# A fused attention and MLP block on one core: requests of the opening in another order, and the first MLP unit's evictions and weight preparation rearranged

## The chip, the cores and the metric

The kernel runs on one core of a Trainium2 chip. The metric is the device time of one execution in microseconds (us), start to end. A core has five instruction streams that run in parallel and meet at semaphores: PE (the matrix engine, with its weight loads listed as PEld), DVE (VectorE), ACT (ScalarE), POOL (GpSimd) and SP (SyncE, which here only issues DMA requests). Each stream issues its own instructions strictly in order: an instruction that waits holds back all that stands behind it on its engine.

## The reference, cut to what matters

The input `A_x` is 2048 rows of 576 columns, float32. Six vectors come from a condition vector `c`; they scale, shift and gate two sub-blocks.

```
mod = (_silu(c) @ w_mod).reshape(c.shape[0], 6, 1, -1)
sa, ca, ga, sb, cb, gb = (mod[:, 0], ..., mod[:, 5])
x = x + ga * _A_ref(_layernorm(x) * (1 + ca) + sa, A_wqkv, A_wo)   # sliding attention, 32 heads, window 256
x = x + gb * _B_ref(_layernorm(x) * (1 + cb) + sb, B_w1, B_w2, B_w3, B_w4)

_B_ref(x):  h  = gelu(layernorm(x) @ w1)              # token mixing
            x1 = x + shifted(h) @ w2
            return x1 + gelu(layernorm(x1) @ w3) @ w4   # channel MLP, 576 -> 4608 -> 576
```

All matrix products are kept near float32 accuracy: each operand is split into a rounded high part and the remainder (low part), and three products (high-high, low-high, high-low) are summed.

## The kernel before

**The order.** The whole program is written as a list of events `at(t, f)`: a number `t` and a function that issues instructions (line 69). `build` sorts the list by `t` and calls the functions in that order (lines 1365 and 1366). The number is only a sort key, not a time on the chip: it decides where the instructions of a function stand in the stream of each engine. Semaphores for the dependences are added by the framework; a tile with `bufs=n` has n buffers in turn, and a write to a reused buffer waits until all readers of the old content are done.

**Opening** (`qkv`, lines 141 to 449). Rows are worked on in four blocks of 512. The first two condition vectors are needed at once (`mod01`); the other four (`modr`, line 222, result `pmr`) are computed while block 0 is on PE, from five tiles `wm` of `w_mod`, 128 x 2304 each, two buffers (`wmload`, line 193; the fifth has 64 rows). They share these two buffers with the tiles `wmf` of `mod01`. For block b, PE computes nine products `qk` of 128 columns each (`fmm`, line 322), 14 matmuls of 512 columns in one of four PSUM banks s0 to s3 in turn. `fev` (line 341) brings each one from PSUM to a tile `qs` (three buffers) with an ACT copy and a DVE subtraction, and `fst` (line 347) stores it to DRAM. On PE, `pmr` of `wm` tile 0 stands between `qk` 4 and `qk` 5 of block 0, that of tile 1 between `qk` 7 and `qk` 8. The weights of Q and K come in three column blocks `raw` (`wload`, two buffers), those of V in two (`vload`, line 271, in the same two buffers, so that the first V load waits until the second block of Q and K weights is split, line 269). All these loads and stores are issued by SP, one behind the other; the rows `x` are loaded by SP from tile 4 on (`xload`, line 157).

**The end of token mixing** (`mixing`, line 983 on; `mix_events`). For each of 16 row tiles t: two products `w` of 288 columns are added to `x1` on DVE (`w2ev`, line 967), the mean and variance are taken on DVE (`st`, result `d{t}mv`), POOL computes the reciprocal root in three small instructions (lines 133 to 136, `d{t}rs`), ACT writes the normalised rows `xm` (line 981), and `rsum` multiplies `x1` by `gb` in place and adds it to the residual `rr`, both on POOL (lines 985 and 986). `rr` is stored to `rd` and comes back later as the start of the MLP's accumulators `acc` (`ainit`, line 1277).

**The MLP** (`mlp`, `mlp_events`). The 4608 hidden columns are taken as 18 units of 2 x 128, first for rows 0 to 1023, then, in reverse, for rows 1024 to 2047. One level of a Strassen-like scheme makes each unit's up-projection seven products instead of eight, in the order P1, P6, P7, P5, P4, P2, P3 (`up`, line 1235), each 7 matmuls of 512 columns. They use banks s0 to s3 in turn, so that P4 needs the bank of P1, P2 that of P6, P3 that of P7, and the next unit's P1 that of P5. P1 is copied to SBUF on ACT (`keep`, line 1212), the others are combined on DVE (`comb`, line 1205: U2 = P6 + U1, U3 = P7 + U2, C22 = P5 + U3, U4 = P5 + U2, C21, C11, C12). Four of them go through gelu and a rounding copy on ACT (lines 1223 and 1225) and a subtraction on DVE (line 1232) to the high and low parts `G`. The down-projection `d` of a unit (line 1255) is interleaved on PE with the next unit's up-projection, and needs `G` and both parts of `W4`.

The weights of unit jj are prepared one unit ahead in one raw tile `wf` with a single buffer, which also holds the rows of `w4` for unit jj-1. In order: nine loads on SP (`wload`, line 1072), four sums on POOL (`wsum`, line 1093), the high parts in two casts on ACT (`whi`, line 1099, slices 0 to 2 and 3 to 6), the low parts in two subtractions on POOL (`wlo`, line 1105) and for a remainder of the rows in two on DVE (`wtail`, line 1113), and for `w4` the multiplication by `gb` on POOL (`w4gb`, line 1119), the cast on ACT (`w4hi`, line 1128) and the low part on POOL (`w4lo`, line 1134). The next `wf` can be loaded only when all of them have read the old one. In `wprep` (line 1137) each has an offset from a start t0 as a fraction of a length dt; for the first two units the events are placed by hand in `mlp_events`:

```
for i, f in enumerate((whi(0, 0, 3), wlo(0, self.nc.gpsimd, 0, 3), whi(0, 3, 7), wlo(0, self.nc.gpsimd, 3, 7))):
    at(Tc + .04 + .01 * i, f)
at(T0 - 7.7, wtail(0, self.nc.vector))
add(wprep(1, 1, 0, T0 - 4.0, 11.0))
```

T0 is the key of the first up-projection, U (24.2) the length of a unit in keys; the first unit's seven products have keys T0 + 0.47 U n / 7.

Of the kernel before, what the change touches and what calls it, by code (L numbers as in the profile page):

```python
# [12 lines left out]
ALU = mybir.AluOpType  # L13
# [7 lines left out]
NT = S // P  # L21
# [12 lines left out]
class Kern:  # L34
# [34 lines left out]
    def at(self, t, f, *a):  # L69
        self.ev.append((t, (lambda: f(*a)) if a else f))  # L70
# [70 lines left out]
    def qkv(self, T0, TB):  # L141
        nc, at, ps = self.nc, self.at, self.ps
# [267 lines left out]
        for b in range(4):  # L410
            t0 = T0 + TB * b
            for f in range(9):
                tf = t0 + fq * f
                if b or f > 2:
                    at(tf, fmm, b, f)
                at(tf + fq + .1, fev, b, f)
                at(tf + fq + 2.0, fst, b, f)
            tv = t0 + 9 * fq
            for i in range(4):
                t = 4 * b + i  # L420
                for r in range(2):
                    at(tv + fv * (i + r / 2), vmm, t, r)
                    at(tv + fv * (i + (r + 1) / 2) + .1, vev, t, r)
                at(tv + fv * (i + 1) + 2.0, vst, t)
            if b == 0:
                at(t0 + 3, wsplit, 2)
                at(t0 + 3.1, vload, 1)
                at(t0 + 7, vsplit, 0, 0)
                at(t0 + 8, vsplit, 0, 1)
                at(t0 + 12, vsplit, 1, 0)  # L430
                at(t0 + 13, vsplit, 1, 1)
                for k in range(5):
                    at(t0 + 4 + 7 * k, wmload, k, 1152, 3456)
                    at(t0 + 16 + 7 * k, modr, k)
                    at(t0 + 17.5 + 7 * k, modre, k)
                at(t0 + 16 + 28 + 4, modst)
            if b < 3:
                for i in range(4):
                    t = 4 * b + 4 + i
                    at(t0 + 2 + i, xload, t)  # L440
                    at(t0 + 14 + 3 * i, st, t)
                    at(t0 + 17 + 3 * i, nrm, t)
                for k in range(5):
                    at(t0 + 31 + 2.5 * k, tr, b + 1, k)
                    at(t0 + 31.6 + 2.5 * k, hev, b + 1, k)
# [360 lines left out]
    def mixing(self, T0, TB):  # L806
        nc, at, ps = self.nc, self.at, self.ps
# [174 lines left out]

        def rsum(t):
            r, x = X["rr", t], X["x1", t]
            nc.gpsimd.tensor_tensor(out=x, in0=x, in1=self.gb, op=ALU.mult)
            nc.gpsimd.tensor_tensor(out=r, in0=r, in1=x, op=ALU.add)

        def xst(t):
            nc.sync.dma_start(self.xmd[t], X["xm", t])
# [5 lines left out]
        for k in range(5):  # L995
# [3 lines left out]
            at(T0 + (8.5, 11, 14.5, 17.7, 22)[k], w2split, k)  # L999
        at(T0 + 24, lambda: nc.sync.dma_start(self.gb, self.modd[5].to_broadcast([P, D])))  # L1000
        return load, tr, tev, w1mm, w1ev, halo, hend, hload, w2mm, w2ev, xpl, st, nrm, rsum, xst, rst

    def mix_events(self, T1, TB, fns):
# [282 lines left out]
    def mlp_events(self, T1, Tc, T0, U, fns):  # L1286
        begin1, begin2, begin3, aload, asum, adup, atr, aev, wload, wsum, whi, wlo, wtail, wprep, w4gb, w4hi, w4lo, ainit, up, down, Ws = fns
        at = self.at
        NJ = F // 2 // P
        SB = S // 1024  # L1290
        B12, B11, B21, B22, T1_, T2, T3, T4 = range(8)
# [8 lines left out]
        add = lambda l: self.ev.extend(l)  # L1300
# [6 lines left out]
        for i, f in enumerate((whi(0, 0, 3), wlo(0, self.nc.gpsimd, 0, 3), whi(0, 3, 7), wlo(0, self.nc.gpsimd, 3, 7))):  # L1307
            at(Tc + .04 + .01 * i, f)
        at(T0 - 7.7, wtail(0, self.nc.vector))
        add(wprep(1, 1, 0, T0 - 4.0, 11.0))  # L1310
        at(T0 + .35, begin3)
        for k in range(8):
            at(T0 + (.2 if k < 5 else .4) * U + .01 * k, ainit(0, (k + 4) % 8))
        t = T0
# [80 lines left out]
```

## Time and profile before

| what | value |
|---|---|
| median of 3 runs | 1800.95 us (1793.26 to 1802.7) |
| the profiled execution's own time | 1797.62 us |
| span of its trace | 1795.5 us |
| mean granted PE clock | 0.98 of full speed |
| opening, up to the last product of block 0 | about 85 us |
| first instruction of the MLP's up-projection on PE | 875.4 us |
| first `d` of the MLP that runs without a break | 899.4 us |

Times in the trace count from the start of the span; the 2.1 us between the span and the execution's own time lie around it. A row of the timeline shows the start, the length, the engine, the line, the operation, output<-input with tile names (buffer numbers left out), shapes and the number of instructions merged in it (x14); in brackets how long the engine had been idle and what ended that. In a row of stretches (windows) stand, for each engine, the busy time and the count, then the granted PE clock, the share of the DMA engines and GB/s. The end of a matmul is modelled; start to start of two rows is the safer measure on PE.

### The profile page before, as it was taken

What the parts mean: (1) busy time and instruction counts of PE and PEld (TensorE: products, weight loads), DVE (VectorE), ACT (ScalarE), POOL (GpSimd) and SP (SyncE); (2) the same over time, 40 slices, a digit from 0 to 9 for tenths busy, and PEclk for the clock granted to TensorE, in tenths of its full rate; (3) what the DMA queues carried; (4) which work ended last, traced back from release to release, by engine and by line L of the source; (5) the groups of instructions that cost most, each with busy time, mean ns of one, the idle gap of its engine ahead of it and who ended that gap; (6) DMA issues with size and microseconds to landing.
All of it is one profiled execution on the core that took longest, in us unless ns stands there. A gap on an engine that the chain in (4) does not pass through costs nothing.

```text
span 1795.5 us, 33620 instructions
## 1 busy us (share of the span) xinstructions
PE 1687.2 (94%) x13369; PEld 1536.9 (86%) x13369; DVE 1105.5 (62%) x1885; ACT 708.4 (39%) x1211; POOL 901.0 (50%) x839
## 2 busy tenths in 40 slices
PE   6999998999999989988799999999989999999998
PEld 4788888888889879988688999999878999999997
DVE  6444255666767637666666666666775666666664
ACT  3222135454544554444334433333433333344331
POOL 4222257545454533464766555556544556655550
PEclk9999999999999999999899999999989999999999
DMA  7755544546455446543422222111233211222211
GB/s 225 277 178 178 173 137 137 146 133 172 129 157 162 140 138 217 196 158 129 158 74 62 62 62 62 48 52 56 62 119 102 62 47 50 59 62 62 62 45 53
DMA packets 156499, 206.77 MB, mean 115 GB/s; under 512 B 19316, under 2 KB 87924, under 8 KB 155768
## 3 DMA queue, kind: packets, MB, share of 16 engines
q1 hardware_dynamic: 153720, 203.19, 36.7%
q8 instruction: 106, 1.74, 0.4%
q10 hardware_dynamic: 2624, 1.45, 0.3%
q14 instruction: 49, 0.40, 0.1%
HBM read 143.76 MB, written 60.56 MB: 114 GB/s over the span
## 4 chain that ended last, share of the span: by engine, by line
PE 74%; DVE 6%; POOL 5%; ACT 5%; issue 4%; DMA 4%; SPq 1%; ACTq 1%; POOLq 0%; DVEq 0%
PE d L1255 24%; PE qk L331 6%; PE X L568 4%; PE mx L519 4%; PE av L607 3%; PE v L369 3%; PE wo L692 3%; PE X L570 2%; PE pg L916 2%; PE w L965 1%; DVE W L1113 1%; ACT avs L612 1%; DMA wmf<-in_w_mod_dram 1%; ACTq L554 1%; DMA wf<-in_B_w_dram 1%
## 5 line engine op out<-in xcount | busy, mean ns | idle before, releaser
L1255 PE MATMUL d<-W,G 128*128 128x288 f32 x3456 | 506.5, 297 | 13.1 <-DVE acc L1263 9.8
L1255 PEld LDWEIGHTS d<-W,G 128*128 128x128 f32 x3456 | 488.3, 189 | 34.9 <-DVE acc L1263 11.0
L1263 DVE TENSOR_TENSOR acc<-d,acc 128x576 f32<-128x576 f32 x288 | 216.9, 754 | 201.3 <-PE d L1255 199.1
L1093 POOL TENSOR_TENSOR wf<-wf 128x384 f32<-128x384 f32 x140 | 144.9, 1055 | 339.8 <-DMA wf<-in_B_w_dram 325.6
L585 ACT ACTIVATE P<-X 128x512 f32<-128x512 f32 (+4 forms) x320 | 177.7, 573 | 195.0 <-PE X L570 153.6
L537 DVE TENSOR_REDUCE m<-mx 128x2 f32<-128x640 f32 x144 | 117.8, 820 | 106.4 <-PE mx L523 105.9
L568 PE MATMUL X<-QD,KS 128*128 128x64 f32 (+2 forms) x704 | 144.7, 298 | 10.6 <-ACT P L585 9.9
L1105 POOL TENSOR_TENSOR W<-wf,W 128x768 fp32r<-128x768 f32 x70 | 152.1, 2194 | 2.7 <-ACT W L1099 2.7
L1232 DVE TENSOR_TENSOR G<-U,G 128x512 fp32r<-128x512 f32 x108 | 91.6, 848 | 100.0 <-ACT G L1225 100.0
L519 PE MATMUL mx<-KD,QS 128*128 128x320 f32 (+4 forms) x512 | 144.3, 342 | 7.0 <-DVE m L537 2.5
L499 POOL TENSOR_SCALAR QS<-QD,rowm 128x512 fp32r<-128x512 f32 x128 | 87.4, 695 | 111.2 <-DMA QD<-qd 73.4
L1223 ACT ACTIVATE U<-U 128x512 f32<-128x512 f32 x108 | 68.5, 634 | 178.6 <-DVE U L1208 178.6
L1223 ACT ACTIVATE C<-C 128x512 f32<-128x512 f32 x36 | 22.8, 634 | 286.4 <-DVE C L1208 286.4
L568 PEld LDWEIGHTS X<-QD,KS 128*128 128x128 f32 x704 | 107.5, 192 | 19.1 <-ACT P L585 16.3
L331 PE MATMUL qk<-hT,Wqk 128*128 128x512 f32 x462 | 110.4, 399 | 1.1 <-DVE qs L345 1.1
L506 POOL TENSOR_SCALAR KS<-KD,rowm 128x768 fp32r<-128x768 f32 (+1 forms) x128 | 109.0, 864 | 0.0
L1119 POOL TENSOR_TENSOR wf<-wf,gb 128x1152 f32<-128x1152 f32 x35 | 104.5, 2985 | 7.1 <-DVE acc L1263 7.1
L331 PEld LDWEIGHTS qk<-hT,Wqk 128*128 128x128 f32 x462 | 87.2, 190 | 24.1 <-DVE qs L345 1.6
L519 PEld LDWEIGHTS mx<-KD,QS 128*128 128x128 f32 x512 | 93.3, 194 | 13.5 <-issue 5.0
L1134 POOL TENSOR_TENSOR W<-wf,W 128x1152 fp32r<-128x1152 f32 x35 | 96.7, 2764 | 6.9 <-ACT W L1128 6.9
L1099 ACT CAST W<-wf 128x1152 fp32r<-128x1152 f32 x70 | 90.1, 1319 | 21.8 <-DMA wf<-in_B_w_dram 10.2
L570 PE MATMUL X<-Mk,identr 128*128 128x256 f32 (+2 forms) x320 | 95.6, 299 | 0.0
(785 smaller groups left out, 3221.6 us busy)
## 6 DMA issues: line engine op xcount, KB each, us to landing
wf<-in_B_w_dram SPq DMA_DIRECT2D x35, 576.0 KB
wf<-in_B_w_dram SPq DMA_DIRECT2D x140, 128.0 KB
KD<-kd SPq DMA_DIRECT2D x72, 216.0 KB
QD<-qd SPq DMA_DIRECT2D x96, 144.0 KB
wf<-in_B_w_dram SPq DMA_DIRECT2D x140, 64.0 KB
qd<-qs SPq DMA_DIRECT2D x16, 512.0 KB
kd<-qs SPq DMA_DIRECT2D x16, 512.0 KB
vd<-Vst SPq DMA_DIRECT2D x16, 312.0 KB
```

Of the source, the lines that this page charges most:

```text
L331: nc.tensor.matmul(po, W[:, a, fs], H[:, c, :], start=(n == 0), stop=(n == 13))
L506: nc.gpsimd.tensor_scalar(t[:, b0:, r], src[:, b0:], M[:, 2 + r:3 + r], 0.0, op0=ALU.mult, op1=ALU.add)
L519: nc.tensor.matmul(pm[:, s, 320 - 64 * nb:320], lhs, K[:, j, 64 * (i + 5 - nb):64 * (i + 5)], start=True, stop=merged(n, j, bb))
L537: nc.vector.tensor_reduce(out=m[:, c:c + 2], in_=pm[:, :, 0:320], axis=mybir.AxisListType.X, op=ALU.max, negate=True)
L568: nc.tensor.matmul(px[:, c:c + q1 - q0], K[:, b + 4].rearrange("p r k -> p (r k)"), Q[:, j, q0:q1], start=(i == 0), stop=False)
L570: nc.tensor.matmul(o, self.identr, mv, start=False, stop=True)
L585: nc.scalar.activation(p[:, lo:], X["px", n, j, k][:, lo:], AF.Exp, scale=SCALE)
L1093: nc.gpsimd.tensor_tensor(out=WF[:, o], in0=WF[:, a], in1=WF[:, b], op=ALU.subtract)
L1105: eng.tensor_tensor(out=W[:, s0:s1, 3:5, :], in0=WF[:, 1 + s0:1 + s1, 0:2], in1=W[:, s0:s1, 0:2, :].bitcast(F32), op=ALU.subtract)
L1119: nc.gpsimd.tensor_tensor(out=R4, in0=R4, in1=gb.unsqueeze(1).to_broadcast([P, 2, D]), op=ALU.mult)
L1255: nc.tensor.matmul(po, G[:, g, ta, b, ts], W[:, w, b, cs], start=(n == 0), stop=(n == 5))
L1263: nc.vector.tensor_tensor(out=a, in0=po, in1=a, op=ALU.add)
```

## The change

Four things, all but one by keys alone. In the opening, the loads of `wm` tiles 0 and 1 and of row tiles 4 and 5 get keys ahead of the V weight loads. In token mixing, `rsum` of row tile 14 runs on DVE. And for MLP unit 1 the call of `wprep` is replaced by events with keys of their own: `keep` of the first product (key T0 + 1.626, unchanged) now comes ahead of the two `whi`, the DVE `wtail` comes behind the second sum U3, and on POOL the two small jobs of row tile 15 and the first `wlo` move ahead of `w4gb`, the second `wlo` ahead of `rsum` of row tile 15. No instruction is added or dropped, and PE's own order does not change.

```diff
                 for k in range(5):
-                    at(t0 + 4 + 7 * k, wmload, k, 1152, 3456)
+                    at(t0 + 4 + 7 * k if k > 1 else -29 + .1 * k, wmload, k, 1152, 3456)
...
-                    at(t0 + 2 + i, xload, t)
+                    at(t0 + 2 + i if t > 5 else -28.9 + .1 * i, xload, t)
...
         def rsum(t):
             r, x = X["rr", t], X["x1", t]
-            nc.gpsimd.tensor_tensor(out=x, in0=x, in1=self.gb, op=ALU.mult)
-            nc.gpsimd.tensor_tensor(out=r, in0=r, in1=x, op=ALU.add)
+            tt = (nc.vector if t == NT - 2 else nc.gpsimd).tensor_tensor
+            tt(out=x, in0=x, in1=self.gb, op=ALU.mult)
+            tt(out=r, in0=r, in1=x, op=ALU.add)
...
         at(T0 - 7.7, wtail(0, self.nc.vector))
-        add(wprep(1, 1, 0, T0 - 4.0, 11.0))
+        at(T0 - 4.0, wload(1, 1, 0))
+        for i, o in enumerate(((T1_, B12, B11), (T2, B22, T1_), (T3, B22, B12), (T4, B21, T2))):
+            at(T0 - 1.8 + .2 * i, wsum(1, *o))
+        pool = self.nc.gpsimd
+        for e, f in ((1.64, whi(1, 0, 3)), (1.66, whi(1, 3, 7)), (1.7, wlo(1, pool, 0, 3)), (1.75, w4gb(0)), (1.8, wlo(1, pool, 3, 7)),
+                     (3.3, w4hi(0)), (3.4, w4lo(0)), (4.9, wtail(1, self.nc.vector))):
+            at(T0 + e, f)
```

The line numbers behind line 984 are higher by one in the new program, those behind line 1310 by seven.

**Opening, SP.** SP's requests from the first V weight load on (`raw_484` or `raw_492`; the last Q and K block stands just ahead of it). Before:

```order
L274 DMA raw_484<-in_A_wqkv_dram 128x4x288
L275 DMA raw_484<-in_A_wqkv_dram 64x288
L276 DMA raw_484<-in_A_wqkv_dram 64x288
L159 DMA x_488<-in_A_x_dram 128x576
L159 DMA x_495<-in_A_x_dram 128x576
L274 DMA raw_497<-in_A_wqkv_dram 128x4x288
L275 DMA raw_497<-in_A_wqkv_dram 64x288
L276 DMA raw_497<-in_A_wqkv_dram 64x288
L195 DMA wm_1152_504<-in_w_mod_dram 128x2304
```

The same place of the changed program:

```order
L195 DMA wm_1152_484<-in_w_mod_dram 128x2304
L195 DMA wm_1152_486<-in_w_mod_dram 128x2304
L159 DMA x_488<-in_A_x_dram 128x576
L159 DMA x_490<-in_A_x_dram 128x576
L274 DMA raw_492<-in_A_wqkv_dram 128x4x288
L275 DMA raw_492<-in_A_wqkv_dram 64x288
L276 DMA raw_492<-in_A_wqkv_dram 64x288
L274 DMA raw_501<-in_A_wqkv_dram 128x4x288
```

Both first `wm` tiles now stand ahead of both V loads; `wm` tile 0 was behind them, and tile 1 five requests further, behind two row tiles and two stores.

**The MLP's first unit, DVE.** From the first half of row tile 15 on (`W_1` is the weight tile of unit 1; `U_0`, `C_0`, `u0P` are sums and products of unit 0). Before:

```order
L969 TENSOR_TENSOR x_15_11684<-w_15_0_11746,x_15_11684 128x288
L969 TENSOR_TENSOR x_15_11684<-w_15_1_11771,x_15_11684 128x288
L130 BN_STATS d15st<-x_15_11684 128x6
L131 BN_STATS d15st<-x_15_11684 128x6
L132 BN_AGGR d15mv<-d15st 128x2
L1113 TENSOR_TENSOR W_1_11635<-wf_11735,W_1_11635 32x7x128 x2
L1208 TENSOR_TENSOR U_0_11850<-u0P_11823,U_0_11831 128x512
L1208 TENSOR_TENSOR U_0_11870<-u0P_11842,U_0_11850 128x512
L1208 TENSOR_TENSOR C_0_11883<-u0P_11862,U_0_11870 128x512
```

After:

```order
L969 TENSOR_TENSOR x_15_11684<-w_15_0_11746,x_15_11684 128x288
L986 TENSOR_TENSOR x_14_11644<-x_14_11644,gb 128x576
L987 TENSOR_TENSOR rr_11651<-rr_11651,x_14_11644 128x576
L969 TENSOR_TENSOR x_15_11684<-w_15_1_11771,x_15_11684 128x288
L130 BN_STATS d15st<-x_15_11684 128x6
L131 BN_STATS d15st<-x_15_11684 128x6
L132 BN_AGGR d15mv<-d15st 128x2
L1209 TENSOR_TENSOR U_0_11846<-u0P_11819,U_0_11827 128x512
L1209 TENSOR_TENSOR U_0_11868<-u0P_11838,U_0_11846 128x512
L1114 TENSOR_TENSOR W_1_11635<-wf_11735,W_1_11635 32x7x128 x2
L1209 TENSOR_TENSOR C_0_11883<-u0P_11860,U_0_11868 128x512
```

The sums U2 and U3 no longer stand behind `wtail`, but C22 does; and the second half of row tile 15 now stands behind `rsum` of tile 14.

**The same stretch, POOL.** From the four `wsum` of unit 1 to `w4lo` of unit 0. Before:

```order
L1093 TENSOR_TENSOR wf_11735<-wf_11735 128x384 x4
L985 TENSOR_TENSOR x_14_11644<-x_14_11644,gb 128x576
L986 TENSOR_TENSOR rr_11651<-rr_11651,x_14_11644 128x576
L1119 TENSOR_TENSOR wf_11735<-wf_11735,gb 128x1152
L133 TENSOR_SCALAR d15rs<-d15mv 128x1
L134 TENSOR_TENSOR d15rs<-d15rs,mhalf 128x1
L136 TENSOR_SCALAR d15rs<-d15mv,d15rs 128x1
L1105 TENSOR_TENSOR W_1_11635<-wf_11735,W_1_11635 128x3x256
L985 TENSOR_TENSOR x_15_11684<-x_15_11684,gb 128x576
L986 TENSOR_TENSOR rr_11701<-rr_11701,x_15_11684 128x576
L1105 TENSOR_TENSOR W_1_11635<-wf_11735,W_1_11635 128x4x256
L1134 TENSOR_TENSOR W_0_11833<-wf_11735,W_0_11833 128x1152
```

After:

```order
L1094 TENSOR_TENSOR wf_11735<-wf_11735 128x384 x4
L133 TENSOR_SCALAR d15rs<-d15mv 128x1
L134 TENSOR_TENSOR d15rs<-d15rs,mhalf 128x1
L136 TENSOR_SCALAR d15rs<-d15mv,d15rs 128x1
L1106 TENSOR_TENSOR W_1_11635<-wf_11735,W_1_11635 128x3x256
L1120 TENSOR_TENSOR wf_11735<-wf_11735,gb 128x1152
L1106 TENSOR_TENSOR W_1_11635<-wf_11735,W_1_11635 128x4x256
L986 TENSOR_TENSOR x_15_11684<-x_15_11684,gb 128x576
L987 TENSOR_TENSOR rr_11701<-rr_11701,x_15_11684 128x576
L1135 TENSOR_TENSOR W_0_11848<-wf_11735,W_0_11848 128x1152
```

The two instructions of tile 14 are gone from POOL, and `w4lo` stands last as before. On ACT, `keep` of unit 0 moves ahead of both `whi` of unit 1, and `xm` of row tile 15 ahead of `w4hi`.

## The prediction

> **What bounds the kernel.** First the shares of the engines and the chain that ended last, from the page:
>
> ```profile
> PE 1687.2 (94%) x13369; PEld 1536.9 (86%) x13369; DVE 1105.5 (62%) x1885; ACT 708.4 (39%) x1211; POOL 901.0 (50%) x839
> PE 74%; DVE 6%; POOL 5%; ACT 5%; issue 4%; DMA 4%; SPq 1%; ACTq 1%; POOLq 0%; DVEq 0%
> ```
>
> PE is busy 94% of the span and carries most of the chain. PE's own work isn't touched, so an edit can gain only where PE stands still or runs at a lower clock. The change touches two such places; everything between and after them follows PE and shifts with it. The first is the opening, PE's timeline:
>
> ```profile
> 38.01 3.54 PE L331 MATMUL qk<-hT,Wqk 128*128 128x512 f32 x14 [1.13 <-DVE qs L345]
> 45.99 2.15 PE L228 MATMUL pmr<-wm,silub 128*32 128x288 f32 x16 [4.44 <-DMA wm<-in_w_mod_dram]
> 48.07 11.12 PE L331 MATMUL qk<-hT,Wqk 128*128 128x512 f32 x42
> 59.12 1.18 PE L228 MATMUL pmr<-wm,silub 128*32 128x288 f32 x16
> 60.23 3.53 PE L331 MATMUL qk<-hT,Wqk 128*128 128x512 f32 x14
> 63.60 2.01 PE L369 MATMUL v<-Wv,hT 128*128 128x288 f32 x14
> ```
>
> Read it start to start: behind `qk` 4 PE stands 4.44 us until `wm` tile 0 has landed, then the first `pmr` takes 2.08 against 1.11 for the second, and `qk` 5 to 7 take 11.05 where `qk` 8 takes 3.37. The stretches give the reason, and SP's timeline why the load is late:
>
> ```profile
> 25.00:30.00 5.00, 5.00 (x23) 4.00 (x23) 3.62 (x5) 4.48 (x6) 3.24 (x3) 1.00 0.00 0
> 46.00:48.10 2.10, 2.10 (x17) 0.62 (x17) 0.00 (x0) 0.00 (x0) 0.00 (x0) 0.50 1.01 363
> 48.10:51.80 3.70, 3.70 (x16) 2.96 (x12) 1.18 (x3) 0.72 (x2) 0.00 (x0) 0.68 1.06 427
> 19.50 1.55 SPq L248 DMA_DIRECT2D raw<-in_A_wqkv_dram  x1
> 32.07 0.37 SPq L274 DMA_DIRECT2D raw<-in_A_wqkv_dram  x1
> 38.98 0.52 SPq L195 DMA_DIRECT2D wm<-in_w_mod_dram  x1
> 40.56 1.42 SPq L352 DMA_DIRECT2D qd<-qs  x2
> ```
>
> After the stall the granted clock is 0.50, then 0.68. SP's last request of the Q and K weights ends at 21.05; then SP stands until 32.07 at the first V load, which waits for its buffer, and the DMA engines are empty (0.00) from 25 to 30. `wm` tile 0 is asked for at 38.98.
>
> The second place is the MLP's first unit: PE, then POOL, DVE, ACT and SP.
>
> ```profile
> 882.66 1.90 PE L1202 MATMUL u0P<-A,W 128*128 128x512 f32 x7 [0.60 <-ACT U L1215]
> 888.65 5.74 PE L1202 MATMUL u0P<-A,W 128*128 128x512 f32 x14 [4.09 <-DVE U L1208]
> 894.22 1.79 PE L1202 MATMUL u1P<-A,W 128*128 128x512 f32 x7
> 899.43 2.27 PE L1255 MATMUL d<-W,G 128*128 128x288 f32 x11 [3.29 <-POOL W L1134]
> ...
> 876.50 4.12 POOL L1093 TENSOR_TENSOR wf<-wf 128x384 f32<-128x384 f32 x4
> 880.58 1.43 POOL L985 TENSOR_TENSOR x<-x,gb 128x576 f32<-128x576 f32 x1
> 882.09 1.42 POOL L986 TENSOR_TENSOR rr<-rr,x 128x576 f32<-128x576 f32 x1
> 883.46 3.46 POOL L1119 TENSOR_TENSOR wf<-wf,gb 128x1152 f32<-128x1152 f32 x1
> 887.01 0.95 POOL L133 TENSOR_SCALAR d15rs<-d15mv 128x1 f32<-128x1 f32 x1
> 888.93 1.84 POOL L1105 TENSOR_TENSOR W<-wf,W 128x768 fp32r<-128x768 f32 x1
> 892.23 1.76 POOL L986 TENSOR_TENSOR rr<-rr,x 128x576 f32<-128x576 f32 x1
> 893.94 2.39 POOL L1105 TENSOR_TENSOR W<-wf,W 128x1024 fp32r<-128x1024 f32 x1
> 896.30 3.07 POOL L1134 TENSOR_TENSOR W<-wf,W 128x1152 fp32r<-128x1152 f32 x1
> 911.68 2.68 POOL L1119 TENSOR_TENSOR wf<-wf,gb 128x1152 f32<-128x1152 f32 x1
> ...
> 875.56 0.46 DVE L969 TENSOR_TENSOR x<-w,x 128x288 f32<-128x288 f32 x1 [1.39 <-PE w L965]
> 876.78 0.21 DVE L132 BATCH_NORM_AGGREGATE d15mv<-d15st 128x2 f32<-128x12 f32 x1
> 882.16 5.71 DVE L1113 TENSOR_TENSOR W<-wf,W 32x896 fp32r<-32x896 f32 x2 [5.17 <-ACT W L1099]
> 887.90 1.49 DVE L1208 TENSOR_TENSOR U<-u0P,U 128x512 f32<-128x512 f32 x2
> 894.66 2.23 DVE L1232 TENSOR_TENSOR G<-U,G 128x512 fp32r<-128x512 f32 x1 [1.36 <-ACT G L1225]
> 876.57 0.87 ACT L981 ACTIVATE xm<-x,d14rs 128x576 f32<-128x576 f32 x1 [4.38 <-POOL d14rs L136]
> 899.40 0.38 SPq L1081 DMA_DIRECT2D wf<-in_B_w_dram  x1
> ```
>
> PE has two waits here. P2 waits 4.09 us for U2, which stands on DVE behind `wtail`; and `d` of unit 0 waits 3.29 us for `w4lo`, the last of a row of POOL jobs without a gap from 876.50 to 899.37. The second ends last. The same end also releases `wf`: SP asks for the next unit's weights at 899.40. So what counts in this place is when `w4lo` ends, not when the products end.
>
> **The change part by part.**
>
> *Opening.* `wm` tiles 0 and 1 and two row tiles are asked for from 21.1 on. Their buffers are free by then: their last readers, the `mod01` products and the first normalisations, come well before 21. By their shapes they are 2 x 1.18 + 2 x 0.29 = 2.95 MB, at the 363 GB/s of the row above 8.1 us, mostly in the time in which the DMA engines are empty. They land near 32, and `pmr` is due at 41.55 (38.01 + 3.54): 9 us to spare. So PE goes on at 41.55. Gained: the 4.44 us of standing; 2.08 - 1.11 = 0.97 at the first `pmr`; 11.05 - 3 x 3.37 = 0.94 at `qk` 5 to 7, since the clock no longer drops. Sum 6.35. What is late next? The 1.13 us ahead of `qk` 4 stay: the DVE work that it waits for isn't moved. `qk` 7 needs the bank of `qk` 3, whose eviction waits for a store (rival B). The V loads stay where they are, since their wait at 32.07 is for a buffer; they have 0.59 MB fewer ahead of them. The Q and K block asked for ahead of the `wm` tiles stays ahead of them in the queue. `wm` tile 2 waits for tile 0's reader and now comes sooner with it. Bounds: 4.44 (the standing alone, if the clock is low all the same) to 6.9.
>
> *`keep` ahead of the casts, `wtail` behind U3.* Takes away the 0.60 (P1 is copied as soon as `xm` 14 is done, 877.44) and the 4.09: U2 and U3 follow the statistics of row tile 15, near 882, so P4, P2 and P3 run through to about 887 with the clock up. On PE that looks like 7 us. But the next product, P1 of unit 1, needs the bank of P5, so C22 and U4, which now stand behind `wtail`; I get it at about 890, against 894.22. And then `d` waits for `w4lo`. All that PE wins ahead of `w4lo` becomes a longer wait there. Taken at nothing by itself.
>
> *POOL.* What moves `w4lo` is POOL's work ahead of it. Two instructions leave, 1.43 + 1.42 = 2.85 us. They go to DVE, and here the rows show a price: a DVE operation on two SBUF operands and a POOL operation don't run together. The `G` subtraction at 894.66 ends at 896.89, right behind POOL's 893.94 job (to 896.33); `wtail` took 5.71 for two, while POOL's multiplication took 3.46 against 2.68 at 911.68, and the small 887.01 job 0.95. So a DVE operation that meets POOL costs it some 0.3 (1.76 - 1.42, 512 columns) to 0.8 us (3.46 - 2.68, 896 columns). For the two of 576 columns I take 0.5 each, nearer to the first.
>
> [...]
>
> The row of POOL jobs, put together again: the sums start at 876.50 and take 4.12 + 2 x 0.5, to 881.6. The `rsum` on DVE can't start before `xm` 14 has read its row (876.57 + 0.87 = 877.44), and holds up the second half of tile 15, at 875.56 before; with two turns of 1.1 to 1.5 us each, that half (0.46) and its statistics (876.99 - 876.02, 1.0 us), d15mv comes between 881.1 and 881.9, about when POOL needs it. Then the three small jobs, 888.93 - 887.01 - 0.7 of waiting = 1.2; `wlo` 1.84; `w4gb` 2.68 and the second `wlo` 2.39, each with 0.8 for a `wtail`; `rsum` of tile 15 2 x 1.42 and `w4lo` 2.7 with one `G` subtraction of 0.35 each. 881.6 + 1.2 + 1.84 + 3.48 + 3.19 + 3.19 + 3.05 = 897.55, against 899.37: 1.8 us sooner. PE, which then waits in the same state as before, and SP's next `wf` load both move by this. SP has the store of `rr` 15 and three accumulator loads ahead of that load; they are done at about the same time, so at most a few tenths are lost. Bounds: 2.85 (no collision) to about -1 (tile 15's statistics late on top).
>
> *Sum.* 6.35 + 1.8 = 8.15. From the profiled execution's own 1797.62 us that gives 1789.5; it stands 3.3 us below the median of the runs shown, from which the same sum gives 1792.8. I say **1791**, between.
>
> **Rivals.**
>
> *A, PE gets its 7 us.* If `d` didn't wait for `w4lo`, it could follow P1 of unit 1, at 892 or 893 in place of 899.4: gain 6.35 + 6.5, about 1785. For: the wait named on PE for longest there is U2. Against: POOL has no gap and its sum can't be 5 us shorter.
>
> *B, a store takes the place of the load.* ACT's row:
>
> ```profile
> 50.00 0.59 ACT L344 CAST qs<-qk 128x512 fp32r<-128x512 f32 x1 [6.49 <-DMA qd<-qs]
> ```
>
> The eviction of `qk` 3 waited for the store asked for at 40.56: 9.4 us. Now `qk` 7 is due at 41.55 + 1.11 + 2 x 3.37 = 49.4. If that store still took 9.4 us, from about 39.8, eviction would end near 50.5: 1.1 us of the gain are lost, with a slower clock perhaps 2; about 1792.5. Against: 1.8 MB of requests ahead of it are gone.
>
> *C, POOL wins nothing.* If DVE's turns cost 1 us each and tile 15's statistics hold POOL up, `w4lo` ends where it did: 6.35 alone, about 1793.
>
> *D, slower: the collision lasts.* In units 1 to 3 `wtail` meets POOL's `wlo`, and PE waits behind it:
>
> ```profile
> 920.01 1.86 PE L1255 MATMUL d<-W,G 128*128 128x288 f32 x12 [1.27 <-DVE acc L1263]
> 945.34 1.86 PE L1255 MATMUL d<-W,G 128*128 128x288 f32 x12 [0.96 <-DVE acc L1263]
> 971.07 1.86 PE L1255 MATMUL d<-W,G 128*128 128x288 f32 x12 [1.38 <-DVE acc L1263]
> ```
>
> From unit 4 on it is gone, because the weights win time on PE from unit to unit. If the new order started them later against PE, it could go on; at 1.2 us a unit, from 7 more units on the kernel is slower than before; for all 13 left in the first half, 1791 + 15.6 = 1806. Against: both still start from `w4lo`.
>
> *E, no effect:* the `wm` loads don't land sooner. Then only the 1.8 are left, about 1797. Against: an empty queue for 5 us.
>
> **How the numbers follow.** Forecast 0.55; A 0.08, B 0.12, C 0.18, D 0.04, E 0.03. The range: down to A, up to 1798, which takes in C, B and E from the median with some spread of runs (1793.26 to 1802.7). About 0.5% is what a measurement of this kernel can tell from no change: 9 us, 1791.9 from the median. The forecast lies on that line: 8.15 is 0.45%, and a median that was drawn high would make it more. So I split it evenly; B and C mostly fall within, A outside: faster 0.47, same 0.50, slower 0.03 (D would need nearly all its units to leave that band).
>
> **What would show it.** Right: no wait of `pmr` on `wm`; the first `pmr` near 41.6 with clock 1.00, and `qk` 8 near 53.9 in place of 60.23; no wait of `u0P` on U; `w4lo` still the releaser of `d`, with an idle of over 4 us, and ending about 8 us sooner than 899.37. DVE's `rsum` of tile 14 should show over 1 us each, where 875.56's 0.46 for 288 columns makes some 0.8 for 576. Wrong: `qk` waiting on stores near 50; `d` released by DVE or ACT; or waits on `acc` beyond unit 4.

## The result, and the profile after

| | before | changed |
|---|---|---|
| median of 17 runs each (lowest to highest) | 1800.77 us (1793.26 to 1804.55) | 1790.52 us (1784.57 to 1794.32) |
| ratio, 95% interval | | 0.9947 [0.9935, 0.9958] |
| profiled execution: own time, span | 1797.62, 1795.5 us | 1794.32, 1792.5 us |

The changed kernel is 9.5 us faster, 7.6 to 11.7 by the interval. Its profiled execution happens to be the slowest of its 17, so the two profiled times differ by 3.3 us only. The traces are therefore compared place by place, each place from a start of its own: the opening from the first `qk` product (22.65 us before, 24.68 after: the last `wmf` tile, for which PE waits in both, let it go on at 18.44 in place of 16.40), and the MLP from POOL's `d13rs`, the reciprocal root of row tile 13 (870.04 and 868.08), which is ahead of all that the change moves there.

The shares of the engines and of the chain, from the page after, hardly move:

```profile
PE 1687.1 (94%) x13369; PEld 1535.6 (86%) x13369; DVE 1103.0 (62%) x1887; ACT 707.3 (39%) x1211; POOL 898.8 (50%) x837
PE 73%; DVE 6%; DMA 5%; POOL 5%; issue 4%; ACT 4%; SPq 1%; ACTq 1%; POOLq 0%; DVEq 0%
```

Two instructions went from POOL to DVE, and PE does the same work. The gain is in PE's waits and, in the opening, in its clock behind the wait. The opening after, PE's timeline and then two rows of SP's:

```profile
40.07 3.54 PE L331 MATMUL qk<-hT,Wqk 128*128 128x512 f32 x14 [1.17 <-DVE qs L345]
43.53 1.18 PE L228 MATMUL pmr<-wm,silub 128*32 128x288 f32 x16
44.64 10.06 PE L331 MATMUL qk<-hT,Wqk 128*128 128x512 f32 x42
54.63 1.18 PE L228 MATMUL pmr<-wm,silub 128*32 128x288 f32 x16
55.74 3.53 PE L331 MATMUL qk<-hT,Wqk 128*128 128x512 f32 x14
...
21.03 2.08 SPq L195 DMA_DIRECT2D wm<-in_w_mod_dram  x2
34.10 0.38 SPq L274 DMA_DIRECT2D raw<-in_A_wqkv_dram  x1
```

The first `pmr` has no bracket any more: it doesn't wait for `wm`. It takes 1.11 start to start in place of 2.08, `qk` 5 to 7 take 9.99 in place of 11.05, and the 1.17 us ahead of `qk` 4 are still there. From the first product to `qk` 8 it is 55.74 - 24.68 = 31.06 us, against 60.23 - 22.65 = 37.58. SP asks for both tiles at 21.03, as soon as the last Q and K block is asked for. Three stretches after:

```profile
25.00:30.00 5.00, 4.37 (x19) 3.25 (x18) 3.94 (x5) 2.96 (x5) 2.27 (x2) 1.00 1.00 365
42.00:45.00 3.00, 3.00 (x25) 1.68 (x24) 0.84 (x3) 1.10 (x3) 0.76 (x1) 1.00 1.04 249
886.00:896.00 10.00, 3.88 (x8) 2.46 (x9) 6.53 (x8) 4.89 (x7) 9.87 (x5) 0.56 0.19 59
```

In the first, the DMA engines, empty before (0.00), are full (1.00, 365 GB/s). In the second, which holds the first `pmr`, the granted clock (third number from the end) is 1.00; around the first `pmr` before it was 0.50. The third belongs to the MLP, where PE now stands, and its clock falls. There PE, then POOL, then DVE:

```profile
877.48 6.80 PE L1203 MATMUL u0P<-A,W 128*128 128x512 f32 x28 [0.25 <-DVE x L969]
888.85 3.33 PE L1203 MATMUL u1P<-A,W 128*128 128x512 f32 x7 [4.57 <-ACT C L1224]
892.11 0.61 PE L1256 MATMUL d<-W,G 128*128 128x288 f32 x1
896.00 3.01 PE L1256 MATMUL d<-W,G 128*128 128x288 f32 x11 [3.28 <-POOL W L1135]
...
868.08 0.22 POOL L133 TENSOR_SCALAR d13rs<-d13mv 128x1 f32<-128x1 f32 x1 [4.97 <-DVE d13mv L132]
874.53 1.02 POOL L1094 TENSOR_TENSOR wf<-wf 128x384 f32<-128x384 f32 x1
876.64 3.24 POOL L1094 TENSOR_TENSOR wf<-wf 128x384 f32<-128x384 f32 x3 [1.09 <-DMA wf<-in_B_w_dram]
882.96 3.46 POOL L1120 TENSOR_TENSOR wf<-wf,gb 128x1152 f32<-128x1152 f32 x1
886.39 3.21 POOL L1106 TENSOR_TENSOR W<-wf,W 128x1024 fp32r<-128x1024 f32 x1
889.55 1.87 POOL L986 TENSOR_TENSOR x<-x,gb 128x576 f32<-128x576 f32 x1
891.51 1.41 POOL L987 TENSOR_TENSOR rr<-rr,x 128x576 f32<-128x576 f32 x1
892.88 3.07 POOL L1135 TENSOR_TENSOR W<-wf,W 128x1152 fp32r<-128x1152 f32 x1
...
875.51 0.76 DVE L986 TENSOR_TENSOR x<-x,gb 128x576 f32<-128x576 f32 x1 [4.51 <-ACT xm L981]
876.30 0.76 DVE L987 TENSOR_TENSOR rr<-rr,x 128x576 f32<-128x576 f32 x1
881.42 5.95 DVE L1114 TENSOR_TENSOR W<-wf,W 32x896 fp32r<-32x896 f32 x2 [1.67 <-ACT W L1100]
```

The 0.60 and the 4.09 us on U are gone: the last four products of unit 0 run through to 884.28. PE then stands 4.57 us ahead of unit 1's first product, whose bank comes free behind `wtail`, C22 and the gelu of C22, and 3.28 ahead of `d`, which still waits for `w4lo`. `w4lo` ends 895.95 - 868.08 = 27.87 us behind `d13rs`, against 899.37 - 870.04 = 29.33. So the two places gave 6.52 and 1.46 us in these two traces.

### The profile page after: what moved, and what is told of

Read it like the earlier page. It is cut to its first block, busy times and chain, and to the rows that moved or that the text cites. A ratio compares the mean times of both kernels' runs of the same rounds, so it can differ in the third digit from the quotient of the medians.

```text
span 1792.5 us, 33622 instructions
## 1 busy us (share of the span) xinstructions
PE 1687.1 (94%) x13369; PEld 1535.6 (86%) x13369; DVE 1103.0 (62%) x1887; ACT 707.3 (39%) x1211; POOL 898.8 (50%) x837
## 4 chain that ended last, share of the span: by engine, by line
PE 73%; DVE 6%; DMA 5%; POOL 5%; issue 4%; ACT 4%; SPq 1%; ACTq 1%; POOLq 0%; DVEq 0%
PE d L1256 24%; PE qk L331 6%; PE X L568 3%; PE v L369 3%; PE mx L519 3%; PE wo L692 3%; PE av L607 3%; PE pg L916 2%; PE X L570 1%; PE w L965 1%; DVE W L1114 1%; DMA wmf<-in_w_mod_dram 1%; DMA or<-od 1%; DMA wf<-in_B_w_dram 1%; ACT avs L612 1%
## 5 line engine op out<-in xcount | busy, mean ns | idle before, releaser
L1264 DVE TENSOR_TENSOR acc<-d,acc 128x576 f32<-128x576 f32 x288 | 216.9, 754 | 205.6 <-PE d L1256 203.2
L1100 ACT CAST W<-wf 128x1152 fp32r<-128x1152 f32 x70 | 90.2, 1318 | 20.5 <-DMA wf<-in_B_w_dram 10.4
```

The costliest lines, as they stand in the source:

```text
L1264: nc.vector.tensor_tensor(out=a, in0=po, in1=a, op=ALU.add)
```

## The experiments

Each kernel was run against the kernel before on the same chip. The table gives, from each profiled run, the distance in us from the first `qk` product to `qk` 8 and to the first product of block 1, and from `d13rs` to the end of `w4lo` and to the first products of units 4 and 8; then the ratio of the times.

| kernel | `qk` 8 | block 1 | `w4lo` | unit 4 | unit 8 | ratio to before, 95% interval |
|---|---|---|---|---|---|---|
| before | 37.58 | 62.15 | 29.33 | 105.97 | 202.37 | |
| changed | 31.06 | 55.64 | 27.87 | 104.46 | 200.86 | 0.9947 [0.9935, 0.9958] |
| changed, again | 31.04 | 55.86 | 27.92 | 105.48 | 201.88 | 0.9945 [0.9928, 0.9962] |
| e1 opening only | 31.23 | 55.90 | 30.45 | 107.09 | 203.49 | 0.9967 [0.9951, 0.9984] |
| e2 MLP only | 36.68 | 61.25 | 28.59 | 104.26 | 200.66 | 0.9992 [0.9977, 1.0008] |
| e3 residual on POOL | 31.04 | 55.61 | 29.73 | 106.95 | 203.35 | 0.9973 [0.9958, 0.9988] |
| e4 old order | 31.01 | 55.58 | 27.32 | 105.20 | 201.60 | 0.9950 [0.9934, 0.9965] |
| e5 residual 15 last | 31.02 | 55.59 | 24.34 | 104.25 | 200.65 | 0.9960 [0.9945, 0.9974] |
| e6 tails later | 31.02 | 55.59 | 27.91 | 105.02 | 201.42 | 0.9963 [0.9949, 0.9978] |
| e7 `wm` 0 only | 31.06 | 56.83 | 28.13 | 105.32 | 201.72 | 0.9964 [0.9948, 0.9980] |
| e9 tails of units 2-4 | 31.51 | 56.07 | 27.65 | 102.17 | 203.02 | 0.9970 [0.9958, 0.9982] |
| e10 e5 and e9 | 31.43 | 56.01 | 24.60 | 100.44 | 199.73 | 0.9978 [0.9964, 0.9992] |
| e11 row tiles old | 31.33 | 55.90 | 27.96 | 104.70 | 201.10 | 0.9949 [0.9933, 0.9965] |
| e12 tails of units 2-17 | 31.07 | 55.63 | 24.73 | 104.02 | 201.05 | 0.9999 [0.9982, 1.0017] |

In a row of the table the opening and the MLP are independent of what happens between them. The five traces with the changed MLP (changed twice, e2, e7, e11) spread by 0.7 us at `w4lo` and by 1.2 at units 4 and 8; so much differs from one trace to the next. From `d13rs` to the end of the trace these five and e4 take 923.2 to 925.0 us, the kernel before 925.4, e1 927.2 and e3 928.8.

Between the opening and the MLP, from the first product of block 1 to `d13rs`, lies work that no edit changes. It takes 781.7 to 790.2 us in the fourteen traces, so a single pair of traces can hide either gain there; but on average it takes 785.8 us in the twelve with the new opening or part of it and 785.5 in the two with the old one (before and e2). So the gain of the opening isn't lost on the way.

### e1 and e2: one half each

e1 keeps only the first two hunks of the change's diff (the keys of `wmload` and `xload`), e2 only the others.

> Only the opening's requests in the new order (wm tiles 0 and 1, row tiles 4 and 5 ahead of the V loads); the MLP and the residual as before. The theory (opening and MLP are two gains that add, 6.5 and 1.5 us in the traces): opening, first product to qk 8 of block 0, 31.1 us against 37.6 before; MLP, from d13rs on POOL to the end of w4lo, 29.3 as before; time against before -6.4 us (ratio 0.9964). Rival 1 (most of the 9.5 us that the time fell comes from the MLP's 4 us wait on U2 that went away): only -3 us or less here (0.9983 or more).

> Only the MLP's new order and the residual of row tile 14 on VectorE; the opening's requests as before. The theory: opening 37.6 us as before, d13rs to the end of w4lo 27.9 us against 29.3; time against before -1.5 to -3 us (ratio 0.9983 to 0.9992). Rival 1 (the products' 7 us count): -6.5 us (0.9964). Rival 2 (nothing is won in the MLP, and what the opening doesn't explain is the spread of the runs): within 0.5 us of before.

Measured: e1 -5.9 us (-8.8 to -2.9), with the opening at 31.23 and the MLP as before (30.45); e2 -1.4 (-4.1 to +1.4), with the opening as before (36.68) and `w4lo` at 28.59. Rival 1 falls: the products' 7 us on PE are not worth 6.5. For e2 alone the interval can't tell 1.5 us from nothing; the trace has 0.7 at `w4lo` and 1.7 at units 4 and 8. Only 0.7 because of the load: in e2 the second sum on POOL could start 9.56 us behind `d13rs`, when its part of `wf` had landed; in the trace before it started at 7.60, without a wait. In e1, with the MLP as before, it was 8.81, and `w4lo` ended 1.1 us later than in the trace before.

### e3 and e4: the residual, or the order

e3 is the changed kernel with tile 14's residual on POOL again:

```diff
-            tt = (nc.vector if t == NT - 2 else nc.gpsimd).tensor_tensor
+            tt = nc.gpsimd.tensor_tensor
```

e4 is the changed kernel with the old keys for unit 1's weights:

```diff
-        at(T0 - 4.0, wload(1, 1, 0))
...
+        add(wprep(1, 1, 0, T0 - 4.0, 11.0))
```

> As the changed kernel, but the residual of row tile 14 back on GpSimd. The theory (what is won in the MLP is won on GpSimd, by the two instructions that left it): w4lo ends 1.5 to 2.6 us later than in the changed kernel, counted from d13rs (29.4 to 30.5 in place of 27.9), though no product waits for U2; time against the changed kernel +1.5 to +2.5 us. Rival 1 (the order of copy, casts and tails is what won): w4lo and time as in the changed kernel, within 0.5 us.

> As the changed kernel, but unit 1's weights prepared by the old keys (casts ahead of the first product's copy, weight tails ahead of the second block sum); the residual of row tile 14 stays on VectorE and the opening stays new. The theory: the product's 4 us wait for U2 is back, yet d13rs to the end of w4lo stays near 27.9 us (27.3 to 28.5) and the time is that of the changed kernel within 0.8 us, since d waits for w4lo either way. Rival 1: +4 us or more against the changed kernel, since the wait on U2 is back.

e3: `w4lo` at 29.73, 1.86 later than in the changed kernel, unit 4 at 106.95 as in the old MLP, and the time -4.9 us, no better than e1's. e4: `w4lo` at 27.32, the time -9.0. In the same set of runs e3's median is 2.8 us above e4's (1795.18 and 1792.41), though the intervals of the two ratios still overlap. Rows of both show why order alone is worth nothing, PE of e3 first, then PE and the DVE tail of e4:

```profile
869.42 11.60 PE L1203 MATMUL u0P<-A,W 128*128 128x512 f32 x49
891.87 0.61 PE L1256 MATMUL d<-W,G 128*128 128x288 f32 x1 [7.08 <-ACT G L1226]
893.79 3.32 PE L1256 MATMUL d<-W,G 128*128 128x288 f32 x11 [1.31 <-POOL W L1135]
...
876.25 1.89 PE L1203 MATMUL u0P<-A,W 128*128 128x512 f32 x7 [1.57 <-ACT U L1216]
879.63 3.53 PE L1203 MATMUL u0P<-A,W 128*128 128x512 f32 x14 [1.48 <-DVE U L1209]
890.06 3.01 PE L1256 MATMUL d<-W,G 128*128 128x288 f32 x11 [4.31 <-POOL W L1135]
875.75 3.10 DVE L1114 TENSOR_TENSOR W<-wf,W 32x896 fp32r<-32x896 f32 x2 [2.04 <-DMA acc<-rd]
```

In e3 all seven products of unit 0 run without a break; then PE stands 7.08 us for `G` and another 1.31 for `w4lo`, which releases `d` 29.8 us behind `d13rs` (864.00). `G` is late for the same reason as `w4lo`: on ACT it stands behind `xm` of row tile 15 and `w4hi`, and in e3 these wait 4.27 and 3.50 us for POOL. In e4 the products wait for U twice (1.57 and 1.48, less than the 4 us expected, since its tail took 3.10 and not 5.71), and `d` is released at 27.4. What was won in the MLP was won by taking two instructions off POOL.

### The changed kernel again, e5 and e6: what is behind `w4lo`

e5 moves the residual of row tile 15 behind `w4lo` on POOL, e6 the tails of unit 1 behind U4 on DVE:

```diff
-            at(s + 7.0, rsum, t)
+            at(s + (7.0 if t < NT - 1 else 7.4), rsum, t)
...
-            at(s + (12.0 if t < NT - 1 else 10.5), rst, t)
+            at(s + (12.0 if t < NT - 1 else 15.4), rst, t)
...
-            at(T0 + (.2 if k < 5 else .4) * U + .01 * k, ainit(0, (k + 4) % 8))
+            at(T0 + (.2 if k < 5 else .48) * U + .01 * k, ainit(0, (k + 4) % 8))
```

```diff
-                     (3.3, w4hi(0)), (3.4, w4lo(0)), (4.9, wtail(1, self.nc.vector))):
+                     (3.3, w4hi(0)), (3.4, w4lo(0)), (6.53, wtail(1, self.nc.vector))):
```

> The changed kernel once more, to stand beside the other kernels of this set on the same chip. Ratio to before 0.9935 to 0.9958 by its first measurement; opening near 31.1 us, d13rs to the end of w4lo 27 to 29 us, the spread coming from when wf's loads land.

> As the changed kernel, but the residual of row tile 15 moved behind w4lo on GpSimd, with its store and three accumulator loads behind the next weight loads on SP. The theory (the end of w4lo sets the MLP's start): its two instructions (1.87 + 1.41 us) leave the way, d13rs to the end of w4lo 24.2 to 25.5 us against 27.9, still the releaser of d; time 2.5 to 3.3 us below the changed kernel. Rival (another engine is as late as w4lo, ScalarE's G or the copy of the next first product): d is released by that and the time falls by less than 1 us. Rival 2 (the accumulators come too late): waits on acc in unit 0, time as the changed kernel or above.

> As the changed kernel, but the weight tails of unit 1 on VectorE behind C22 and U4 instead of ahead of them. The theory: the first product of unit 1 comes some 4 us sooner on the tensor engine (near 884 in place of 888.85) and the wait for w4lo gets longer by as much; d13rs to the end of w4lo stays within 0.6 us, the time within 0.8 us of the changed kernel. Rival (the products' place counts): -2 us or more.

e6 did what was expected in the trace: unit 1's first product came 16.78 us behind `d13rs` in place of 20.8, and `w4lo` and unit 4 stayed. Its time is 3.2 us above the changed kernel's in the same set (1800.35 x (0.9963 - 0.9945)); the two intervals overlap, and the trace has no place for it.

e5 is a miss. `w4lo` came 3.5 us sooner as expected, and `d` followed without a wait. But unit 4 came only 0.2 to 1.2 us sooner, and the time is 2.7 us above the changed kernel's (the intervals overlap here too). `d` is no longer released by `w4lo`, as the theory had it: it stands directly behind unit 1's first product, which comes hardly sooner (20.5 us behind `d13rs`, 20.8 in the changed kernel). Besides the residual, e5 also moves its store and three accumulator loads, as the last two hunks show. PE's waits in units 1 to 3 of e5, and the tails on DVE of units 2 and 3:

```profile
897.27 1.06 PE L1256 MATMUL d<-W,G 128*128 128x288 f32 x6 [0.69 <-DVE acc L1264]
911.09 1.85 PE L1256 MATMUL d<-W,G 128*128 128x288 f32 x12 [0.72 <-DVE acc L1264]
938.71 3.25 PE L1256 MATMUL d<-W,G 128*128 128x288 f32 x12 [3.29 <-DVE acc L1264]
...
904.79 4.25 DVE L1114 TENSOR_TENSOR W<-wf,W 32x896 fp32r<-32x896 f32 x2
929.85 6.83 DVE L1114 TENSOR_TENSOR W<-wf,W 32x896 fp32r<-32x896 f32 x2
```

A tail that meets POOL's subtractions took 6.83 us; one that meets none took 2.19 (e12, below). The three waits add up to 4.70 us, against 3.00 in the changed kernel. The likely reason, read from the rows: `w4lo` lets PE go on sooner while the next weights are no further, so PE meets the collision harder.

### e9 and e10: the tails of units 2 to 4 out of the way

```diff
-                          (t0 + 0.50 * dt, whi(jj, 3, 7)), (t0 + 0.62 * dt, wtail(jj, nc.vector)),
+                          (t0 + 0.50 * dt, whi(jj, 3, 7)), (t0 + (0.80 if 1 < jj < 5 else 0.62) * dt, wtail(jj, nc.vector)),
```

e9 is the changed kernel with this edit, e10 is e5 with it.

> As the changed kernel, but the weight tails of units 2 to 4 on VectorE stand behind the block sum C21 of the unit before, instead of ahead of C22. The theory (in units 1 to 3 the tails meet GpSimd's weight subtractions and hold up VectorE, so the tensor engine waits for acc): the waits on acc there (0.26 + 1.12 + 1.62 us in the changed kernel) go, the weights have 8 us to spare; d13rs to the first product of unit 4 102 to 103 us against 104.3 to 105.5; time 2 to 3 us below the changed kernel. Rival (the collision only moves to the next operation on VectorE, G or acc): waits of the same sum at another place, time within 1 us.

> The later tails of units 2 to 4 together with the residual of row tile 15 behind w4lo. The theory (w4lo's 3.5 us, won when that residual moved alone, were lost again at unit 2's tail, which took 6.83 us and made the tensor engine wait 3.29 us on acc): now they are kept; d13rs to the end of w4lo near 24.3 us, to the first product of unit 4 99 to 101 us; time 4 to 6 us below the changed kernel. Rival (the weight chain itself, load to w4lo, paces units 1 to 3): first product of unit 4 not before 102.5 us and waits on W in their place.

The first product of unit 4 comes where it was expected, 102.17 and 100.44, though waits for `acc` of 1.29 and 2.36 us are left ahead of it. Then unit 5's tail, at its old place, met POOL, and PE waited there. Rows of e9, DVE and PE:

```profile
981.76 6.20 DVE L1114 TENSOR_TENSOR W<-wf,W 32x896 fp32r<-32x896 f32 x2
990.00 2.95 PE L1256 MATMUL d<-W,G 128*128 128x288 f32 x12 [2.67 <-DVE acc L1264]
```

At unit 8 e9 is 1.8 us later than the mean of the changed MLP's five traces (201.24), and its time is 3.8 us above e11's, below, which has the changed kernel's time and was run in the same set (1799.22 x (0.9970 - 0.9949)). The reading that fits is that the waits of units 1 to 3 are how the weights win their lead: PE falls back until the tails no longer meet POOL, and an edit that spares the waits leaves the lead unwon. No run shows the lead itself. e10 is 1.5 us sooner at unit 8, and yet its time is some 5 us above e11's (1799.22 x (0.9978 - 0.9949)). Its trace has no place for that: from `d13rs` to the end it takes 924.9 us, like the changed kernel (923.6 and 924.4), and of the 7.8 us by which its trace is longer than e11's 6.4 lie ahead of `d13rs`, and so ahead of all that was changed in the MLP. Why its other runs are slower too is left open.

### e12: all tails of the first half

e12 is e10 with `1 < jj < 18`.

> The residual of row tile 15 behind w4lo and the weight tails of units 2 to 17 (all that are left of the first half) behind C21. With the tails moved for units 2 to 4 alone, unit 5's tail, back at its old place, took 6.18 us and the tensor engine waited 2.64 us on acc: the collision had only been put off, since the weights had not yet won their lead. The theory: with all tails moved no such wait is left; d13rs to the first product of unit 8 196 to 198 us, against 199.7 with units 2 to 4 alone and 200.9 to 201.9 in the changed kernel; time 2.5 to 4.5 us below the changed kernel (near 1786 to 1788). Rival 1 (what the trace gains at the MLP's start is lost again elsewhere, as the times of the two kernels with later tails say, which were 3 to 4 us above the changed kernel): 1791 us or more although unit 8 comes early. Rival 2 (the tails meet the next thing on VectorE in every unit): waits on acc from unit to unit, unit 8 not before 201 us.

Rival 2 is what came: unit 8 at 201.05, later waits for `acc` of 0.3 to 0.8 us in one unit after another, and the time that of the kernel before. DVE and PE of e12 in unit 9:

```profile
1112.35 2.82 DVE L1233 TENSOR_TENSOR G<-C,G 128x512 fp32r<-128x512 f32 x1
1115.80 2.19 DVE L1114 TENSOR_TENSOR W<-wf,W 32x896 fp32r<-32x896 f32 x2
1118.84 1.85 PE L1256 MATMUL d<-W,G 128*128 128x288 f32 x12 [0.77 <-DVE acc L1264]
```

Now the `G` subtraction meets POOL (2.82 us, alone 0.69), the tail stands behind it, and `acc` comes too late. From unit 8 to unit 17 PE needs 222.0 us, in the changed kernel 216.9. No version tried beats the changed kernel.

### e7 and e11: which of the opening's requests

e7 asks early for `wm` tile 0 alone, e11 for both `wm` tiles but not for the row tiles:

```diff
-                    at(t0 + 4 + 7 * k if k > 1 else -29 + .1 * k, wmload, k, 1152, 3456)
+                    at(t0 + 4 + 7 * k if k > 0 else -29, wmload, k, 1152, 3456)
...
-                    at(t0 + 2 + i if t > 5 else -28.9 + .1 * i, xload, t)
+                    at(t0 + 2 + i, xload, t)
```

(e7 has both hunks, e11 the second only.)

> As the changed kernel, but of the opening's loads only wm tile 0 is asked for early; tile 1 and the row tiles 4 and 5 keep their old place behind the V loads. The theory (one late load made both the stall and the half clock): opening 31.1 us as in the changed kernel (30.9 to 31.6), time within 0.8 us of it. Rival (the row of loads is what counts: tile 1 then comes late): pmr of tile 1 waits on wm ahead of qk 8, opening 32.5 us or more.

> As the changed kernel, but row tiles 4 and 5 are asked for at their old place; both wm tiles stay early. The theory (of the opening's loads the row tiles are worth 1.2 us of their own: with only wm tile 0 early, the statistics of row tile 7 came 1.45 us later and a transpose of block 1 waited 1.27 us on VectorE): that wait is back, the products of block 1 start 1.0 to 1.3 us later from the first product on than in the changed kernel (56.7 to 57.0 in place of 55.63 us), the opening to qk 8 still 31.1 us. Rival (it was wm tile 1's later load): no such wait, 55.6 to 55.9 us.

In e7 the opening to `qk` 8 is 31.06, as expected, and tile 1 comes in time. But block 1 starts 0.8 to 1.3 us later than in the kernels that ask for both tiles early, and the time is 3.4 us above the changed kernel's in the same set, where 0.8 at most was expected (the intervals overlap). The theory of e11 put the late block 1 down to the row tiles; e11 shows that it isn't so: with the row tiles late and both `wm` tiles early, block 1 starts at 55.90 and the time is that of the changed kernel. The rival holds: it is tile 1. Rows of e7: SP with tile 1's request, one ACT eviction, PE; then that eviction in the changed kernel:

```profile
42.15 0.89 SPq L352 DMA_DIRECT2D qd<-qs  x2
43.13 1.14 SPq L195 DMA_DIRECT2D wm<-in_w_mod_dram  x1
44.37 6.07 SPq L352 DMA_DIRECT2D qd<-qs  x2
54.74 0.59 ACT L344 CAST qs<-qk 128x512 fp32r<-128x512 f32 x1 [1.86 <-PE qk L331]
73.81 0.66 PE L306 MATMUL pt<-ident,xh 128*128 128x128 f32 x4 [1.27 <-DVE macc L235]
...
52.60 0.58 ACT L344 CAST qs<-qk 128x512 fp32r<-128x512 f32 x1
```

Tile 1's request, 1.14 us of SP's time and 1.18 MB, stands between the Q stores; the eviction is 2.1 us later (54.74 against 52.60), DVE's work behind it too, and a transpose of block 1 waits 1.27 us for DVE in place of 0.17. The eviction's bracket names PE, but PE's products run at the same times in both; what it waits for is then most likely the store that frees its buffer. That path is read from the rows; what the runs show is that tile 1's place is worth about 1 us at block 1, though its data comes in time either way.

## Why the prediction was right

The mechanism came out as predicted: a late load and the clock behind it in the opening, and in the MLP the end of `w4lo`, not the products. That 1791 and 1790.52 us lie so close is luck: 1791 is a choice between two starting times, and the forecast gain of 8.15 us, taken from the median of 17 runs, gives 1792.6. Two terms also met their numbers in part by luck: the opening's because tile 1 was moved along, and POOL's because two errors cancelled.

- **Opening, 6.35.** Measured 6.52 in the two traces (e2's opening, the same as before, was 0.9 us shorter than that trace's: 5.6). All three parts are there: 4.44 of standing, 0.97 at the first `pmr`, 1.06 at `qk` 5 to 7. `qk` 8 is at 55.74; less the 2.03 us by which the first `qk` started later it is 53.7, for 53.9 predicted. What the sum lacked is what e7 lost, about 1 us: "what is late next" was asked of PE's banks and not of SP's queue. Had only the load that was waited for been moved, the forecast would have been about 1 us too good.
- **`keep` and `wtail` worth nothing by themselves.** Shown by e4 (the old order, the same time) and e3 (the new order, no gain at `w4lo`). PE's idle was foreseen as one wait of over 4 us for `w4lo`; it came as 4.57 ahead of unit 1's first product and 3.28 ahead of `d`.
- **POOL, 1.8.** Measured 1.46. The collisions were sized well: `w4gb` took 3.46 and the second `wlo` 3.21 (predicted 3.48 and 3.19). Two errors cancelled at the sums: tile 14's residual on DVE cost POOL next to nothing there (three sums took 3.24 us, 2.97 in the second trace; its own turns took 0.76 each, for over 1 predicted), since POOL was standing for `wf` just then; but that wait, 1.09 us, was not foreseen. Where `wf` landed early, the predicted price is seen: in e4, e5 and e9 the four sums took 5.06 to 5.07 us in one go, for 4.12 before, 0.95 for the predicted 2 x 0.5. The `G` subtraction shows it from DVE's side: 2.82 us in e12 where it meets POOL, 0.69 alone. A sum on DVE with one operand from a product (`u0P`) shows no such price: in the trace before, one took 0.68 us at 896.81 with POOL in `w4lo` (896.30 to 899.37) all the while.
- **The sign "`w4lo` about 8 us sooner than 899.37".** It ended at 895.95. The sign was badly put: it took for granted that all between the two places shifts with PE, but in these two traces PE's lead over the trace before wanders between 7.3 us ahead and 1.2 behind on the way. Each gain counted from a start of its own, it holds: 6.52 + 1.46 = 7.98.
- **The sum, 8.15, against 9.5 (7.6 to 11.7).** The two halves alone gave 5.9 and 1.4, together 7.3, each with an interval of some 3 us to either side. The sum lies in all of these; whether the last 1.4 us have a cause isn't settled.
- **The rivals.** A fell with e1 and e2; its 1785 was counted from the lower of the two starting times, from the one that gives 1791 it is 1786.3. E fell in the opening, where the tile had landed in time. C is what e3 shows, and needs the residual on POOL. B: the eviction of `qk` 3 still waited for a store, but it started at 48.55, and `qk` 7 needs the bank only at 44.64 + 2 x 3.33 = 51.3:

```profile
48.55 0.59 ACT L344 CAST qs<-qk 128x512 fp32r<-128x512 f32 x1 [2.88 <-DMA qd<-qs]
```

- **Rival D.** The collisions lasted no longer than before. The waits for `acc` were 3.00 us in units 1 to 3 (3.61 before), and there were none in the rest of the first half:

```profile
916.18 1.85 PE L1256 MATMUL d<-W,G 128*128 128x288 f32 x12 [0.26 <-DVE acc L1264]
941.63 1.86 PE L1256 MATMUL d<-W,G 128*128 128x288 f32 x12 [1.12 <-DVE acc L1264]
967.62 1.86 PE L1256 MATMUL d<-W,G 128*128 128x288 f32 x12 [1.62 <-DVE acc L1264]
```

D's mechanism, a tail that meets POOL where PE runs close to its weights, is what the rows show in e5 and e9.

## What to carry to other kernels

Follow a wait to what would be waited for next, on every queue that the step touches: 4.7 us of PE's waits for U were worth nothing here because `w4lo` came behind them, and a request moved out of a store queue was worth about 1 us that no wait had named. Waits that end by themselves after a few units can be the way in which a producer wins its lead; taking them away puts them off. Compare two traces from a start of their own at each place, since what lies between shifts them by more than the change is worth.

## What the runs showed of the hardware

In the traces before and after, PE's granted clock fell to 0.50 in pieces of 3.41, 6.83, 10.24 and 13.65 us, all multiples of 3.41 (the last piece of each runs into the end of the trace), and it fell behind short stands too. In the trace before, PE stopped at 41.55. Two windows of 3.41 us each of the trace before, and two of the trace after in attention:

```profile
40.18:43.59 3.41, 1.37 (x6) 0.75 (x4) 1.46 (x2) 1.77 (x4) 1.37 (x2) 1.00 1.09 357
43.59:47.00 3.41, 1.01 (x12) 0.44 (x16) 1.43 (x2) 0.00 (x0) 1.27 (x1) 0.50 0.90 275
...
265.90:269.31 3.41, 2.21 (x16) 2.04 (x17) 2.13 (x5) 2.04 (x5) 1.06 (x2) 1.00 0.82 228
269.31:272.72 3.41, 3.41 (x17) 3.41 (x17) 1.26 (x3) 1.24 (x3) 3.01 (x4) 0.50 0.17 53
```

The clock was down 2.04 us after PE had stopped, behind a window in which PE had been busy 1.37 of 3.41 us; and in attention behind one with 2.21 of 3.41, with no single stand over 1.1 us in it. So in both places the clock fell behind a window in which PE was idle for a part only. No clean limit came out: the window in attention was busy 0.65 of its length, while one that was busy 0.46 (1.57 of 3.41 us, from 859.82 in the trace after) was followed by one with full clock (1.00).

Which places of attention and mixing lose clock differs from run to run: the profiled run before has half clock from 227.9, 828.7, 856.0 and 866.2, the one after from 269.3 and 313.7 instead. Summed over a profiled run, (1 - clock) x time is 37.4 us before, 33.9 in the changed kernel's (1794.32 us), 30.0 in its second (1788.21), 26.5 in e11's (1785.59) and 42.5 in e12's (1807.5). Over the 17 runs of the changed kernel, those with a mean clock of 0.986 or 0.987 took 1784.57 to 1786.27 us, those with 0.978 to 0.980 took 1791.79 to 1794.01. Most of the spread of this kernel's times goes with it (the correlation of time and mean clock over the 17 runs is -0.86), and a single profiled run can't tell 3 us.
